# A layer norm, a feed-forward pass and a long convolution on one core: block 0's transposes and first products in halves of 256 rows

## The chip, the core and the metric

The kernel runs on one core of a Trainium2 chip. The metric is device time in microseconds (us) of one execution; for each kernel the median over its runs is compared. The core has a matrix engine (TensorE, PE in the profile, its weight loads PEld), VectorE (DVE), ScalarE (ACT), GpSimd (POOL) and SyncE (SP), each of which works through its own list of instructions strictly in order, and 16 DMA engines. DMAs are issued by SP, ACT or POOL from the same lists.

## What is computed

The input is x (2048 rows of 576 features). With xn = layernorm(x), the result is

```
out = x + q(xn) * y(k, v) + relu(xn @ w1) @ w2        # w1 is 576 x 4608, w2 is 4608 x 576
```

where y is a gated long convolution over the 2048 rows (short shift convolution of k, times v, then a causal convolution of length 2048 done as a transform written in matmuls) and xn gates it. All data are float32. The change concerns only the feed-forward part, relu(xn @ w1) @ w2, in its first microseconds.

## The kernel before, in words

**Precision.** A float32 product is made of three fast passes: each operand is split into a rounded high part (`hi`, `h1`, `hh`, written by ACT) and a low part (the operand minus its high part, written by DVE for activations and by POOL for weights), and high*high, low*high and high*low are summed in PSUM.

**Tiles of the feed-forward part.** The rows are 16 tiles of 128, in 4 blocks of 4 tiles (512 rows). The 4608 hidden features are 12 chunks of 384, each chunk 3 feature tiles j of 128. The loops run over halves of the rows (blocks 0 and 1, then 2 and 3), then chunks `ci`, then the blocks of the half, then j. `mm1` (L323) makes one hidden tile: 14 matmuls of 512 columns into a PSUM tile `psh` (two buffers), from the transposed activations `xhi`, `xlo`, `xhl` and the split weights h, l; then ACT writes `hh` (relu, L333) and DVE `ll` (L334). `mm2` (L340) multiplies the three hidden tiles of a chunk by w2: for each row tile and each half of the 576 output columns 9 matmuls of 288 columns into `pso` (three buffers), added to the accumulator `acc` by DVE (L355 for block 0, with a factor rstd; L359 for the others).

**The convolution** is a generator (`conv`). After a given amount of matmul work `tick` (L719) lets it emit its next few instructions, so that its matmuls stand among those of the feed-forward part.

**The start.** `acc` first holds x itself. Row tiles are loaded in pairs, each pair by two DMAs of 64 partitions (L152). The loads ahead of everything are, in this order: pair 0 (tiles 0, 1) and pair 2 (tiles 2, 3), each with one DMA on SP's queue and one on ACT's; then on SP's queue the first 128 columns of w1's chunk 0 (L282, L284, three DMAs), its other 256 columns (three DMAs), w2's chunk 0 (L292), the pairs of block 1 and the convolution's kernel. A DMA on SP can't be issued before the eighth DMA ahead of it has landed, because eight semaphores go round. 22 + 11 matmuls on a tile of zeros (`keep_warm`, L749) keep PE busy while it has nothing to do.

`first_xT` (L210) prepares block 0. For each of its four row tiles DVE takes the statistics (L168, L169), writes the negated mean (L225), and ACT subtracts the mean (L227; tile 1 is done by DVE, L189); the factor rstd is left to L355. PE transposes each centred tile in five pieces (L233), and when all four row tiles stand in the five PSUM tiles, `split_x` (L200) makes `xhi` and `xlo`/`xhl` for c = 0 to 4, 512 columns at a time. `split_w1` (L294) splits a feature tile of w1: ACT writes h (L301), POOL l (L271). `split_w2` (L303) does the same for w2 (L310, L271). After the first hidden tile, `make_xT` (L242) prepares block 1: statistics, rstd, then (x - mean) * rstd by DVE (L183), transposes (L263), split.

**What sets the order.** Within an engine the order is fixed when the program is built, by a list scheduler with its own estimate of times; `tc.issue_after(i)` only says that what stands inside is not placed ahead of instruction i. PE thus alternates between hidden tiles 0 and 1 from the first product on: the two are finished together, six `pso` matmuls follow, then hidden tile 2.

Of the kernel before, what the change touches and what calls it, by code (L numbers as in the profile page):

```python
# [10 lines left out]
F32 = mybir.dt.float32  # L11
F32R = mybir.dt.float32r
AF = mybir.ActivationFunctionType
OP = mybir.AluOpType
# [23 lines left out]
A2 = U * T  # L38
GR = P // (2 * A2)
NG = A1 // GR  # L40
N_WARM = 22
WARM_TILE = (0, 6, 3, 2)


W_MM1 = 14 * 512
# [63 lines left out]
def h3_ffn_kernel(ctx: ExitStack, tc, x, k, v, shift_k, ssm_k, ssm_D, w1, w2, fwd, inv, mid, out):  # L109
# [76 lines left out]
    def centred(dst, src, t):  # L186


        return nc.vector.tensor_scalar(dst, src, mv[:, t, 0:1], None, op0=OP.subtract)  # L189

    xT = {}
    done = {}

# [3 lines left out]
        hl = xp.tile([P, 512], F32R, tag="xhl", name=f"xhl{b}")  # L197
        xT[b] = (hi, lo, hl)

    def split_x(b, c, ps):  # L200
        hi, lo, hl = xT[b]
        if c < 4:
            nc.scalar.activation(hi[:, c, :], ps, AF.Copy)
            nc.vector.tensor_tensor(lo[:, c, :], ps, hi[:, c, :], OP.subtract)  # L204
        else:
            done["act"] = nc.scalar.activation(hl[:64, :], ps[:64, :], AF.Copy)
            done["dve"] = nc.vector.tensor_tensor(hl[64:, :], ps[:64, :], hl[:64, :],
                                                  OP.subtract)

    def first_xT(srcs):  # L210

        xT_tiles(0)
        ps = []
        for c in range(5):
            ps.append(ps_o.tile([P, 512], F32, tag="o", name=f"psx{c}") if c >= 3 else fft_psum())
        neg = xp.tile([P, BT], F32, tag="neg", name="neg", bufs=1)
        behind = None
        for t in range(BT):
            if t % 2 == 0:
                pair = xp.tile([P, 2, D], F32, tag="xn", name=f"xn{t}", bufs=BT // 2)  # L220
            xn = pair[:, t % 2, :]
            with tc.issue_after(behind.ins) if behind else nullcontext():
                stats(t, srcs[t])
                if t != 1:
                    behind = nc.vector.tensor_scalar(neg[:, t:t + 1], mv[:, t, 0:1], -1.0, None,  # L225
                                                     op0=OP.mult)
                    done["act"] = nc.scalar.activation(xn, srcs[t], AF.Identity,  # L227
                                                       bias=neg[:, t:t + 1])
                else:
                    behind = centred(xn, srcs[t], t)  # L230
            for c in range(5):
                w = min(P, D - c * P)
                nc.tensor.transpose(ps[c][:w, t * P:(t + 1) * P], xn[:, c * P:c * P + w], ident)  # L233
            keep_warm(WARM_TILE[t])
        with tc.issue_after(done["act"].ins):
            split_w1(0, 1)
        for c in range(5):
            split_x(0, c, ps[c])
        with tc.issue_after(done["dve"].ins):
            inv_std(0, BT)  # L240

    def make_xT(b, srcs, in_place=False):  # L242

        xT_tiles(b)
        t0 = b * BT
        with tc.issue_after(done["acc" if in_place else "dve"].ins):
            for t in range(t0, t0 + BT):
                stats(t, srcs[t])
            inv_std(t0, BT)
        xn = []  # L250
        for t in range(t0, t0 + BT):
            if in_place:
                xn.append(srcs[t])
            else:
                if t % 2 == 0:
                    pair = xp.tile([P, 2, D], F32, tag="xn", name=f"xn{t}", bufs=BT // 2)
                xn.append(pair[:, t % 2, :])
            normalized(xn[-1], srcs[t], t)
        for c in range(5):
            w = min(P, D - c * P)  # L260
            ps = fft_psum()
            for i in range(BT):
                nc.tensor.transpose(ps[:w, i * P:(i + 1) * P], xn[i][:, c * P:c * P + w], ident)  # L263
            split_x(b, c, ps)

    def at_turn(ci):
# [48 lines left out]
    hid = {}  # L315
    added = set()

    def mm1(ci, b, j):
        h1, l1, _, _ = weights[ci][j]
        hi, lo, hl = xT[b]  # L320
        ps = ps_h.tile([P, 512], F32, tag="h", name=f"psh{ci}_{b}_{j}")
        seq = []
        for c in range(4):  # L323
            seq += [(h1[:, c, :], hi[:, c, :]), (h1[:, c, :], lo[:, c, :]),
                    (l1[:, c, :], hi[:, c, :])]
        seq += [(h1[:, 4, :], hl), (l1[:, 4, :], hl)]
        for i, (a, m) in enumerate(seq):
            nc.tensor.matmul(ps, a, m, start=i == 0, stop=i == len(seq) - 1)  # L328
            if i % 7 == 6:
                tick(W_MM1 / 2)  # L330
        hh = hp.tile([P, 512], F32R, tag="hh", name=f"hh{ci}_{b}_{j}")
        ll = hp.tile([P, 512], F32R, tag="ll", name=f"ll{ci}_{b}_{j}")
        done["act"] = nc.scalar.activation(hh, ps, AF.Relu)  # L333
        nc.vector.scalar_tensor_tensor(ll, ps, 0.0, hh, op0=OP.max, op1=OP.subtract)  # L334
        hid[ci, b, j] = (hh, ll)

    def mm2(ci, b, i):
        t = b * BT + i
        cols = slice(i * P, (i + 1) * P)
        if ci == HALVES * NCHUNK - 1:  # L340
            while t not in added:
                next(stream)
        for h in range(2):
            ps = ps_o.tile([P, 512], F32, tag="o", name=f"pso{ci}_{t}_{h}")
            dc = slice(h * NH, (h + 1) * NH)
            n = 0
            for j in range(FT):
                hh, ll = hid[ci, b, j]
                _, _, h2, l2 = weights[ci][j]
                for a, m in ((hh, h2), (hh, l2), (ll, h2)):  # L350
                    nc.tensor.matmul(ps[:, :NH], a[:, cols], m[:, dc],  # L351
                                     start=n == 0, stop=n == 3 * FT - 1)
                    n += 1
            if b == 0:
                done["acc"] = nc.vector.scalar_tensor_tensor(  # L355
                    acc[t][:, dc], ps[:, :NH], rstd[:, t:t + 1], acc[t][:, dc],
                    op0=OP.mult, op1=OP.add)
            else:
                done["acc"] = nc.vector.tensor_tensor(acc[t][:, dc], ps[:, :NH], acc[t][:, dc],  # L359
                                                      OP.add)  # L360
            if ci == HALVES * NCHUNK - 1 and t == T - 1:
                for u, queue in ((0, nc.sync), (1, nc.scalar)):
                    queue.dma_start(out[u, :, t, dc], acc[t][halves(u)[0], dc])
            tick(W_MM2 / 2)
        if ci % NCHUNK == NCHUNK - 1:
            if t < HT:
                if t % 2:
                    nc.sync.dma_start(fin[t // 2], pairs[t - 1])
            else:
                if t == T - 2:  # L370
                    move(acc[t], out, t, store=True)
                elif t % 2 and t < T - 1:
                    move(pairs[t - 1], out, slice(t - 1, t + 1), store=True)
# [375 lines left out]
    def keep_warm(n):  # L749
        for i in range(n):  # L750
            nc.tensor.matmul(idle, warm[:, :P], warm, start=True, stop=True)

    keep_warm(N_WARM)
    split_w1(0, 0)
    first_xT(acc)
    for j in range(2, FT):
        with tc.issue_after(done["act"].ins):
# [21 lines left out]
    for half in range(HALVES):  # L779
        for cc in range(NCHUNK):  # L780
            ci = half * NCHUNK + cc
            for bi in range(HB):
                b = half * HB + bi
                if half == 0 and cc == NCHUNK - 1:
                    tl = {}
                    bn = HB + bi
                    for t in range(bn * BT, (bn + 1) * BT, 2):
                        pair = load_x(t, "xn", BT // 2)
                        tl[t], tl[t + 1] = pair[:, 0, :], pair[:, 1, :]
                    make_xT_later = (bn, tl, True)  # L790
# [47 lines left out]
```

## Time and profile before

| | |
|---|---|
| median of 3 runs | 1081.67 us (1080.42 to 1083.54) |
| the profiled execution | 1082.52 us, of which its span, first to last instruction, is 1080.7 us |
| granted clock of PE in the span | 1.000 |
| PE busy in 0 to 20 us, 20 to 40 us | 18.33 us, 18.55 us |
| PE busy in 40 to 60, 60 to 80, 80 to 100 us | 20.00 us each |
| bytes moved by DMA | 150.79 MB, 140 GB/s over the span |

A row of the profile's timeline gives start and length in us, engine, line, operation, `out<-in`, shape and count; in brackets stands how long the engine was idle before and what ended that. A page's groups give busy time and the mean length of one instruction in ns. The busy time of PE counts the length of a matmul, though the next one starts before it ends.

### The profile page before, as it was taken

The numbers are of one execution on the slowest core, as the hardware profiler recorded it, in microseconds if no ns is written. First come the engines' busy times: TensorE is split into PE (matmuls) and PEld (weight loads), VectorE is DVE, ScalarE is ACT, GpSimd is POOL, SyncE is SP. The second block draws the span as 40 slices with busy tenths as digits, with TensorE's granted clock in tenths as the row PEclk, the third lists the DMA queues.
The fourth block names the chain that finished last, engine by engine and source line by source line (L and its number), as shares of the span: only waits on it lengthen the run. The fifth ranks groups of instructions, "written<-read, shape, count | busy, mean of one in ns | idle before, by whom it ended". The sixth has DMA issues, their size and how long they took to land.

```text
span 1080.7 us, 17268 instructions
## 1 busy us (share of the span) xinstructions
PE 1068.9 (99%) x6545; PEld 975.2 (90%) x6545; DVE 728.8 (67%) x1215; ACT 583.2 (54%) x1181; POOL 322.1 (30%) x307
## 2 busy tenths in 40 slices
PE   8999999999999999999999999999999999999998
PEld 5989998989999999999989999899999999999998
DVE  6322787849998767677556575666656656877774
ACT  4221787823442423333387887888788864543430
POOL 4341342423423422412313041312224032442410
PEclk9999999999999999999999999999999999999999
DMA  9960455665545425416644342434344237644524
GB/s 231 182 158 1 149 156 163 196 184 151 178 134 151 150 75 156 126 51 201 187 145 138 97 149 86 136 99 136 97 142 133 86 103 224 203 126 145 170 76 110
DMA packets 99183, 150.79 MB, mean 140 GB/s; under 512 B 45261, under 2 KB 49583, under 8 KB 99100
## 3 DMA queue, kind: packets, MB, share of 16 engines
q1 hardware_dynamic: 79548, 92.87, 29.7%
q0 software_dynamic: 19232, 56.08, 17.7%
q8 instruction: 52, 0.85, 0.3%
q10 hardware_dynamic: 320, 0.74, 0.3%
q14 instruction: 31, 0.25, 0.1%
HBM read 114.26 MB, written 35.39 MB: 138 GB/s over the span
## 4 chain that ended last, share of the span: by engine, by line
PE 90%; DMA 5%; ACT 2%; DVE 2%; issue 1%; SPq 0%; POOL 0%; POOLq 0%; ACTq 0%; DVEq 0%
PE pso L351 39%; PE psh L328 39%; PE psf L555 7%; PE psf L391 3%; DMA r<-in_w 2%; DMA acc<-in_x 1%; PE psf L693 1%; PE psf L694 1%; DMA sk<-in_shift_k 1%; PE psf L263 1%; DMA zk<-zk 1%; DMA k<-in_k 0%; ACT h L310 0%; DVE lok L546 0%; POOL l L271 0%
## 5 line engine op out<-in xcount | busy, mean ns | idle before, releaser
L271 POOL TENSOR_TENSOR l<-r,h 128x640 fp32r<-128x640 f32 (+1 forms) x144 | 225.3, 1569 | 550.3 <-ACT h L301 397.9
L351 PE MATMUL pso<-l,hh 128*128 128x288 f32 x1152 | 338.3, 295 | 0.0
L351 PE MATMUL pso<-h,ll 128*128 128x288 f32 x1152 | 337.8, 295 | 0.0
L351 PE MATMUL pso<-h,hh 128*128 128x288 f32 x1152 | 336.6, 295 | 0.8 <-DVE acc L359 0.6
L328 PE MATMUL psh<-xhi,h 128*128 128x512 f32 x576 | 225.9, 393 | 1.6 <-DVE ll L334 1.2
L328 PE MATMUL psh<-xlo,h 128*128 128x512 f32 x576 | 226.2, 393 | 0.0
L328 PE MATMUL psh<-xhi,l 128*128 128x512 f32 x576 | 225.5, 391 | 0.0
L351 PEld LDWEIGHTS pso<-h,hh 128*128 128x128 f32 x1152 | 215.6, 188 | 7.4 <-DVE acc L359 1.0
L351 PEld LDWEIGHTS pso<-l,hh 128*128 128x128 f32 x1152 | 216.1, 188 | 5.9
L351 PEld LDWEIGHTS pso<-h,ll 128*128 128x128 f32 x1152 | 215.8, 188 | 0.5
L333 ACT ACTIVATE hh<-psh 128x512 fp32r<-128x512 f32 x144 | 85.4, 595 | 173.5 <-PE psh L328 172.8
L359 DVE TENSOR_TENSOR acc<-pso,acc 128x288 f32<-128x288 f32 x288 | 128.4, 451 | 72.1 <-PE pso L351 69.1
L334 DVE SCALAR_TENSOR_TENSOR ll<-psh,hh 128x512 fp32r<-128x512 f32 x144 | 98.9, 687 | 102.6 <-ACT hh L333 102.0
L328 PEld LDWEIGHTS psh<-xhi,l 128*128 128x128 f32 x576 | 108.2, 188 | 20.4
L328 PEld LDWEIGHTS psh<-xhi,h 128*128 128x128 f32 x576 | 108.0, 188 | 17.5 <-DVE ll L334 1.4
L328 PEld LDWEIGHTS psh<-xlo,h 128*128 128x128 f32 x576 | 108.1, 188 | 15.5 <-DVE xlo L204 0.4
L310 ACT ACTIVATE h<-r 128x576 fp32r<-128x576 f32 x72 | 48.6, 681 | 57.1 <-DMA r<-in_w 32.9
L355 DVE SCALAR_TENSOR_TENSOR acc<-pso,rstd,acc 128x288 f32<-128x288 f32 x96 | 48.4, 513 | 33.4 <-PE pso L351 32.7
L392 ACT ACTIVATE zx<-psf 128x288 f32<-128x288 f32 x64 | 25.7, 407 | 61.5 <-PE psf L391 37.5
L385 DVE TENSOR_TENSOR ks<-kt,ks 64x288 fp32r<-64x288 f32 x64 | 57.2, 893 | 2.4 <-ACT ks L384 0.4
L591 DVE TENSOR_TENSOR k<-psf,k 128x288 f32<-128x288 f32 x64 | 29.2, 456 | 42.8 <-ACT sw L590 42.6
L328 PE MATMUL psh<-xhl,l 128*128 128x512 f32 x144 | 56.4, 392 | 0.0
(109 smaller groups left out, 1533.7 us busy)
## 6 DMA issues: line engine op xcount, KB each, us to landing
r<-in_w POOLq DMA_DIRECT2D x23, 864.0 KB, 6.0
r<-in_w POOLq DMA_DIRECT2D x23, 768.0 KB, 6.5
zk<-zk SPq DMA_DIRECT2D x32, 288.0 KB, 2.8
zx<-zx SPq DMA_DIRECT2D x32, 288.0 KB, 3.1
ztk<-zk SPq DMA_DIRECT2D x32, 288.0 KB, 3.1
ztx<-zx SPq DMA_DIRECT2D x32, 288.0 KB, 2.8
zy<-vo SPq DMA_DIRECT2D x32, 288.0 KB, 2.0
zo<-zy SPq DMA_DIRECT2D x32, 288.0 KB, 3.0
```

The source lines that it names most:

```text
L271: return nc.gpsimd.tensor_tensor(dst, src, hi, OP.subtract)
L310: nc.scalar.activation(h2, r2[:, j, :], AF.Copy)
L328: nc.tensor.matmul(ps, a, m, start=i == 0, stop=i == len(seq) - 1)
L333: done["act"] = nc.scalar.activation(hh, ps, AF.Relu)
L334: nc.vector.scalar_tensor_tensor(ll, ps, 0.0, hh, op0=OP.max, op1=OP.subtract)
L351: nc.tensor.matmul(ps[:, :NH], a[:, cols], m[:, dc], start=n == 0, stop=n == 3 * FT - 1)
L355: done["acc"] = nc.vector.scalar_tensor_tensor(acc[t][:, dc], ps[:, :NH], rstd[:, t:t + 1], acc[t][:, dc], op0=OP.mult, op1=OP.add)
L359: done["acc"] = nc.vector.tensor_tensor(acc[t][:, dc], ps[:, :NH], acc[t][:, dc], OP.add)
L385: nc.vector.tensor_tensor(dst[other], src[own], dst[own], OP.subtract)
L391: nc.tensor.matmul(ps[:, :NH], w[:, u, n, :], stk, start=n == 0, stop=n == 1)
L555: nc.tensor.matmul(ps[:, :NH], a, m[:, cols], start=n == 0, stop=n == 2)
L591: nc.vector.tensor_tensor(k1[:, cols], ps, k1[:, cols], OP.mult)
```

## The change

Block 0 is handled in two halves of 256 rows. In each half two row tiles are centred and transposed, the five PSUM tiles are split 256 columns at a time, and the products of hidden tiles 0 and 1 (`N_EARLY = 2`) for those 256 columns are made: 14 matmuls of 256 columns for each, high-weight products first and low-weight products (which need POOL's l) last. `mm1` then finds these two `psh` tiles ready and only writes hh and ll.

- In a half, the first row tile is centred by DVE (statistics, then subtract); the second by ACT alone, which sums the row in one pass with an accumulated output and subtracts in a second one. Its statistics, still needed for rstd, are taken by DVE later.
- Pair 0 alone is loaded ahead of w1. Pair 2 is issued on SP's queue between the first 128 and the other 256 columns of w1's chunk 0 (inside `load_w1`).
- h of feature tile 0 is split behind tile 1's centring; h of feature tile 1 behind the third high part (c = 2) of the first half; w1's third feature tile and w2's three come after the second half, as before.
- There are 21 + 2 matmuls on zeros instead of 33.
- Block 1 (`second_xT`) is prepared after hidden tile 1 instead of hidden tile 0. Its statistics follow the first low part `ll`; its tiles are centred only, by ACT with a negated mean from DVE, and rstd is left to `mm2`, so that L355's form of the addition (L414 in the changed kernel) serves block 1 too.
- Blocks 2 and 3 keep `make_xT`, in place.

```diff
-N_WARM = 22
-WARM_TILE = (0, 6, 3, 2)
+N_WARM = 21
+N_EARLY = 2
...
+    def centre(dst, src, t, how, behind=None):
+        if how != "dve":
+            neg = xp.tile([P, 1], F32, tag="neg", name=f"neg{t}", bufs=4)
+        with tc.issue_after(behind.ins) if behind else nullcontext():
+            if how == "act":
+                nc.scalar.activation(dst, src, AF.Copy, scale=-1.0 / D, accum_out=neg)
+            else:
+                stats(t, src)
+                if how == "dve":
+                    return nc.vector.tensor_scalar(dst, src, mv[:, t, 0:1], None,
+                                                   op0=OP.subtract)
+                last = nc.vector.tensor_scalar(neg, mv[:, t, 0:1], -1.0, None, op0=OP.mult)
+            act = nc.scalar.activation(dst, src, AF.Identity, bias=neg)
+        return act if how == "act" else last
...
     def first_xT(srcs):
...
+        xn = row_pairs(0)
+        behind = {0: None, 1: None}
+        for half in range(2):
+            cols = slice(256 * half, 256 * half + 256)
+            for i in range(2):
+                t = 2 * half + i
+                last = centre(xn[t], srcs[t], t, ("dve", "act")[i], behind[i])
+                if t == 0:
+                    with tc.issue_after(last.ins):
+                        stats(1, srcs[1])
+                transposes(ps, xn[t], t)
+            if half == 0:
+                keep_warm(2)
+                with tc.issue_after(last.ins):
+                    split_w1(0, 0)
             for c in range(5):
...
+                high, low = split_x(0, c, ps[c], cols)
+                if half == 0 and c == 2:
+                    behind[0] = low
+                    with tc.issue_after(high.ins):
+                        split_w1(0, 1)
+            behind[1] = high
+            for j in range(N_EARLY):
+                if half == 0:
+                    early[j] = ps_h.tile([P, 512], F32, tag="h", name=f"psh0_0_{j}")
+                products(0, 0, j, early[j], cols)
+        with tc.issue_after(low.ins):
+            stats(3, srcs[3])
+
+    def second_xT(srcs):
+        xT_tiles(1)
+        with tc.issue_after(lows[0].ins):
             inv_std(0, BT)
+        xn = row_pairs(BT)
+        last = lows[1]
+        for i in range(BT):
+            last = centre(xn[i], srcs[BT + i], BT + i, "both", last)
...
+            split_x(1, c, ps)
+        with tc.issue_after(last.ins):
+            inv_std(BT, BT)
...
     def load_w1(ci):
...
+            if step == P:
+                load_acc(2)
...
+    def products(ci, b, j, ps, cols=None):
...
+        if cols is None:
+            seq = [p for c in range(5) for p in (*highs[2 * c:2 * c + 2], rests[c])]
+        else:
+            seq = highs + rests
         for i, (a, m) in enumerate(seq):
-            nc.tensor.matmul(ps, a, m, start=i == 0, stop=i == len(seq) - 1)
+            to, m = (ps, m) if cols is None else (ps[:, cols], m[:, cols])
+            nc.tensor.matmul(to, a, m, start=i == 0, stop=i == len(seq) - 1)
...
+    def mm1(ci, b, j):
+        if ci == b == 0 and j in early:
+            ps = early[j]
+            tick(W_MM1)
...
-            if b == 0:
+            if b < HB:
                 done["acc"] = nc.vector.scalar_tensor_tensor(
...
-    for t in range(0, BT, 2):
-        load_acc(t, queues=(nc.sync, nc.scalar))
+    load_acc(0, queues=(nc.sync, nc.scalar))
...
-                    if (ci, b, j) == (0, 0, 0):
-                        make_xT(1, acc)
+                    if (ci, b, j) == (0, 0, 1):
+                        second_xT(acc)
```

More of the change, by code (lines that the diff above doesn't have):

```diff
@@ L215, in first_xT @@
             ps.append(ps_o.tile([P, 512], F32, tag="o", name=f"psx{c}") if c >= 3 else fft_psum())
[L216 to L230, printed above, removed]
-            for c in range(5):
-                w = min(P, D - c * P)
-                nc.tensor.transpose(ps[c][:w, t * P:(t + 1) * P], xn[:, c * P:c * P + w], ident)
-            keep_warm(WARM_TILE[t])
@@ L235, in first_xT @@
[L235 to L239, printed above, removed]
-            inv_std(0, BT)
[L242 to L258, printed above, removed]
+        xn = row_pairs(0)
@@ L263, in make_xT @@
                 nc.tensor.transpose(ps[:w, i * P:(i + 1) * P], xn[i][:, c * P:c * P + w], ident)
+            split_x(1, c, ps)
+        with tc.issue_after(last.ins):
+            inv_std(BT, BT)
+    def make_xT(b, srcs):
+        xT_tiles(b)
+        t0 = b * BT
+        with tc.issue_after(done["acc"].ins):
+            for t in range(t0, t0 + BT):
+                stats(t, srcs[t])
+            inv_std(t0, BT)
+        for t in range(t0, t0 + BT):
+            normalized(srcs[t], srcs[t], t)
+        for c in range(5):
+            w = min(P, D - c * P)
+            ps = fft_psum()
+            for i in range(BT):
+                nc.tensor.transpose(ps[:w, i * P:(i + 1) * P], srcs[t0 + i][:, c * P:c * P + w],
+                                    ident)
             split_x(b, c, ps)
@@ L333, in mm1 @@
         done["act"] = nc.scalar.activation(hh, ps, AF.Relu)
-        nc.vector.scalar_tensor_tensor(ll, ps, 0.0, hh, op0=OP.max, op1=OP.subtract)
+        lows.append(nc.vector.scalar_tensor_tensor(ll, ps, 0.0, hh, op0=OP.max,
+                                                   op1=OP.subtract))
         hid[ci, b, j] = (hh, ll)
@@ L753, in h3_ffn_kernel @@
     keep_warm(N_WARM)
-    split_w1(0, 0)
     first_xT(acc)
```

45 lines of the change are left out of this document (28 added, 17 removed).

## The prediction

> **What bounds the kernel now.** I read the page's busy times first, then the windows, then the timeline of the start.
>
> ```profile
> span 1080.7 us, 17268 instructions
> PE 1068.9 (99%) x6545; PEld 975.2 (90%) x6545; DVE 728.8 (67%) x1215; ACT 583.2 (54%) x1181; POOL 322.1 (30%) x307
> ```
>
> PE is the bound: 11.8 us of the span are not its own. What happens ahead of the steady stretch is worth what it moves that stretch, and the change works only there. The timeline of the start:
>
> ```profile
> 1.20 8.74 PE L751 MATMUL psw<-warm 128*128 128x512 bf16 x32 [1.20 <-DVE table L745]
> 4.59 4.85 PEld L751 LDWEIGHTS <-warm 128*128 128x128 bf16 x23 [0.27 <-issue]
> 6.08 0.82 DVE L168 BATCH_NORM_STATS2 bn<-acc 128x6 f32<-128x288 f32 x2 [4.93 <-DMA acc<-in_x]
> 6.93 0.21 DVE L169 BATCH_NORM_AGGREGATE mv<-bn 128x2 f32<-128x12 f32 x1
> 8.34 0.52 DVE L189 TENSOR_SCALAR xn<-acc,mv 128x576 f32<-128x576 f32 x1
> 8.66 0.37 SPq L292 DMA_DIRECT2D r<-in_w  x1
> 9.92 0.74 ACT L301 ACTIVATE h<-r 128x640 fp32r<-128x640 f32 x1 [1.78 <-DMA r<-in_w]
> 10.56 1.43 ACT L227 ACTIVATE xn<-acc,neg 128x576 f32<-128x576 f32 x2
> 11.90 0.72 ACT L301 ACTIVATE h<-r 128x640 fp32r<-128x640 f32 x1
> 12.53 1.54 ACT L203 ACTIVATE xhi<-psf 128x512 fp32r<-128x512 f32 x3
> 12.70 1.56 POOL L271 TENSOR_TENSOR l<-r,h 128x640 fp32r<-128x640 f32 x1 [0.41 <-ACT h L301]
> 13.13 1.89 DVE L204 TENSOR_TENSOR xlo<-psf,xhi 128x512 fp32r<-128x512 f32 x3 [1.96 <-ACT xhi L203]
> 13.15 0.74 PE L328 MATMUL psh<-xhi,h 128*128 128x512 f32 x2 [0.34 <-ACT xhi L203]
> 15.54 1.83 ACT L310 ACTIVATE h<-r 128x576 fp32r<-128x576 f32 x3
> 15.73 4.35 POOL L271 TENSOR_TENSOR l<-r,h 128x640 fp32r<-128x640 f32 x3 [1.47 <-ACT h L301]
> 19.65 1.09 ACT L333 ACTIVATE hh<-psh 128x512 fp32r<-128x512 f32 x2 [2.07 <-PE psh L328]
> 20.30 0.40 PE L351 MATMUL pso<-h,hh 128*128 128x288 f32 x1 [0.23 <-ACT hh L333]
> 21.84 0.68 DVE L334 SCALAR_TENSOR_TENSOR ll<-psh,hh 128x512 fp32r<-128x512 f32 x1
> 22.58 0.50 PE L328 MATMUL psh<-xhi,h 128*128 128x512 f32 x1 [1.22 <-DVE ll L334]
> ```
>
> Products start at 13.15 us, hidden tiles 0 and 1 end near 20, and hidden tile 2 waits until 22.58 for `ll`, which frees its PSUM buffer. Up to there the two kernels do the same: the transposes of block 0, 28 products, six `pso` matmuls. So I compare one moment: **the first product of hidden tile 2, at 22.58 us before**. From then on the chain of waits is PE alone:
>
> ```profile
> 22.58 3.47 PE psh L328 x14
> 26.04 1.59 PE pso L351 x12
> 27.64 1.31 PE psf L263 x12
> 28.95 1.20 PE pso L351 x9
> 43.46 3.20 PE psh L328 x14
> ```
>
> These also give prices: 3.20/14 = 0.229 us for a matmul of 512 columns, 1.59/12 = 0.133 for 288, 1.31/12 = 0.109 for a transpose. A straight line through the first two gives 0.119 for 256 columns; the 288-column price 0.133 is the upper bound, half of 0.229 the lower. I take 0.119 (only 32 columns away from a measured one): the 56 half products then cost 6.7 us against 28 x 0.229 = 6.4.
>
> **When the data come.** SP's windows (clock, DMA share, GB/s at the end of a row):
>
> ```profile
> 2.00:4.00 2.00, 1.00 0.92 226
> 4.00:6.00 2.00, 1.00 1.06 242
> 6.00:8.00 2.00, 1.00 1.03 202
> 8.00:10.00 2.00, 1.00 1.15 302
> 10.00:12.00 2.00, 1.00 1.08 346
> ```
>
> The DMA engines are full throughout, so what counts is the order of the bytes. A pair of x is 0.59 MB, w1's first part 0.33, its second 0.66. Before: two pairs and the first part, 1.51 MB, are through at 8.5 us, and ACT could use them at 9.92 (1.78 us of idle until a DMA), a lag of about 1.3 us. With the second part it is 2.16 MB, through at 10.6, usable about 11.8; ACT's next split of w1 at 11.90 shows no DMA wait. After: pair 0 first, as before, usable at 6.08; w1's first part behind 0.92 MB, through at 5.9, usable at about 7.2 instead of 9.9; pair 2 behind 1.51 MB, usable at about 9.8; **w1's second part behind the same 2.16 MB, so again at about 11.8**. SP's three DMAs of that part and pair 2's two are issued several us before their turn; w2's load, issued at 8.66 before, when pair 2 had landed, now waits for w1's first part instead (7.2) and has 2.16 MB ahead of it either way.
>
> **The first half.** DVE: statistics 6.08 to 7.14, subtraction to about 7.7 (0.52, L189). ACT beside it: a pass that sums, then a pass that subtracts. Before shows no accumulating pass; its bounds are the 681 ns of a plain 128x576 ACTIVATE (below) and twice that; I take 0.70, near the plain one. The second pass is 0.76 (two in 1.43, overlapping): done at 7.6, at the upper bound at 8.3, when PE is still transposing tile 0. The matmuls on zeros run at 0.42 us until 4.59, then at 0.21 (4.85/23), so 23 end at about 7.8; ten transposes end at 8.9. The ten matmuls left out filled idle time and bring nothing by themselves.
>
> ```profile
> L310 ACT ACTIVATE h<-r 128x576 fp32r<-128x576 f32 x72 | 48.6, 681 | 57.1 <-DMA r<-in_w 32.9 <-PE pso L351 24.1
> L392 ACT ACTIVATE zx<-psf 128x288 f32<-128x288 f32 x64 | 25.7, 407 | 61.5 <-PE psf L391 37.5 <-issue 21.6 <-ACT h L310 1.2
> ```
>
> A high part of 256 columns costs ACT, in a row, between half of 0.51 (1.54/3, 512 columns) and 0.41 (288 alone); I take 0.31, a low part on DVE 0.37 (half of 1.89/3 is 0.32, L359 below takes 0.45 for 288). ACT's order in the changed program is: the two passes, h of tile 0, high parts c = 0, 1, 2, **h of tile 1**, high parts c = 3, 4, two passes for row tile 3, five high parts of the second half, h of tile 2, w2's three h, then hh. So h of tile 0 runs 7.7 to 8.4, three high parts 8.7 to 9.7, and then ACT stands until w1's second part lands at 11.8. **This is the wait that takes the place of the old ones.** Queued behind it on ACT are c = 3 and 4 and all of the second half; behind those low parts on DVE, the subtraction of row tile 2 (whose statistics wait for pair 2 only); on PE, five products of tile 0 are done at 10.1, and the next in its list needs h of tile 1. From 10.1 to 12.55 PE has nothing.
>
> **From 11.8 to the moment compared.** h of tile 1 to 12.5 (0.72). PE: 19 half products at 0.119, to 14.8 (POOL's l of tile 1, 12.6 + 1.56 = 14.2, is needed at 14.4). ACT ends c = 4 at 13.2, row tile 3's passes at 14.7; DVE ends row tile 2 at 14.4: both in time. Ten transposes to 15.9; the first PSUM tile is whole at 15.6. ACT: five high parts 15.7 to 17.2, h of tile 2 to 17.9, w2's three (1.83) to 19.7, hh at 19.6 to 20.2. PE follows the low parts (last at 18.0) and ends its 28 at about 19.4, so it waits for hh: the `pso` matmuls begin at 20.25, as before (20.30). Three run; the other three need w2's first l. POOL: l of tile 2 from 17.95, then that l, 1.55 + 1.4 (4.35 for three): 20.95. They end at 21.4. `ll` has freed the buffer by 20.9. **Hidden tile 2 starts at 21.4 instead of 22.58: 1.2 us.** The stall of 1.22 us goes because DVE no longer has block 1's statistics ahead of `ll`; late next are POOL's l and ACT's w2 splits.
>
> **Block 1.** DVE now does, between 21 and 28: second `ll`, four statistics, four negated means, third `ll`; ACT two tiles (23.2 to 25.5) before hh, two behind it. PE's first six transposes (due 26.2) find theirs; the last three (due 28.3) wait for the fourth tile, which DVE's queue (statistics of 1.05 and `ll` 0.7) gives at about 28.6: 0.3 us. DVE's four L183 (2.2 us) leave. Between no loss and 0.35, the gain is 0.85 to 1.2; **I take 1.0.**
>
> **Costed at nothing.** L355's form for block 1 (rows: 513 against 451 ns, 96 more) is 6 us of DVE in 1080, hidden behind PE (DVE busy 67%); without cover 6 us. POOL is 2.4 us later with w1's next chunk: its split stood for 16 us. Two ticks fewer only move convolution steps.
>
> ```profile
> L359 DVE TENSOR_TENSOR acc<-pso,acc 128x288 f32<-128x288 f32 x288 | 128.4, 451 | 72.1 <-PE pso L351 69.1
> L355 DVE SCALAR_TENSOR_TENSOR acc<-pso,rstd,acc 128x288 f32<-128x288 f32 x96 | 48.4, 513 | 33.4 <-PE pso L351 32.7
> 41.52 4.63 POOL L271 TENSOR_TENSOR l<-r,h 128x640 fp32r<-128x640 f32 x3 [16.16 <-ACT h L301]
> ```
>
> The profiled execution was 1082.52 us (span 1080.7 and 1.8 around it), 0.85 above the median. It becomes 1081.5, and the median of 1081.67 becomes **1080.7 us**.
>
> **Rivals.**
>
> *A: ACT does not wait for w1's second part.* If it were there by 9.7, h of tile 1 would run 9.65 to 10.4, the high parts end at 11.0, row tile 2 on DVE at 12.6, the transposes at 13.7, the second half at 17.3, and hidden tile 2 would start at about 19.2: a gain of 3.4, **1078.3**. For it: weights move at 302 to 346 GB/s, pairs of x at 202 to 242. Against it: 2.16 MB must be through, whatever their order, and were not before 10.6.
>
> *B: PE's clock drops in the hole; slower than before.* Between 7.8 and 12.55 PE has ten transposes and five half products. At the start it took 3.4 us (1.20 to 4.59) of matmuls at 0.42 us until they came at 0.21. If that returns once, 3.4 us at half speed from 12.55 delay the first half's end by 1.7, and all behind it: 1.7 - 1.0, **1082.4**. If it lasts two such periods, 3.4 are lost: **1084.1**. It decides if so little work in 4.7 us counts as idle. Against it: before, from 9.8 to 13.15, PE also had only transposes and one matmul on zeros, and the 28 products behind came at full speed (13.15 to 20, 28 x 0.229 = 6.4). For it: that stretch was shorter and denser. [...]
>
> *C: the later order.* The scheduler moves convolution steps everywhere. PE's waits behind 60 us are
>
> ```profile
> PE psf L555 <- ACT k L579: 1.7, 3, 0.8
> PE psf L391 <- ACT zk L392: 1.5, 1, 1.5
> PE psf L555 <- DVE k L591: 0.7, 2, 0.6
> PE pso L351 <- DVE acc L359: 0.6, 1, 0.6
> ```
>
> 4.5 us in sum; all gone is 1076.2, all doubled 1085.2. No row says which way.
>
> **Chances.** Forecast 0.52, A 0.20, B 0.16, C 0.12 (half each way). A measurement of this kernel tells about 0.3% from no change, 3.2 us: faster means below 1078.4, slower above 1084.9. A lies on the first edge (0.12 of it beyond), C's halves add 0.06 each, B's upper part with noise 0.05: faster 0.18, within 0.71, slower 0.11. The likeliest case alone reaches from 1079.5 to 1082; with A and most of B the range is 1077.8 to 1084.2.
>
> **What would show it.** ACT's split of feature tile 1 (L345) idle for about 2 us until a DMA, starting near 11.8; 256-column matmuls 0.119 apart; the first product of hidden tile 2 near 21.4, `pso` held by POOL just ahead of it. Under A that split starts before 10.5 and hidden tile 2 near 19; under B half products come 0.21 or more apart behind 12.5. I am wrong if the second part lands elsewhere than at 11.8, if an accumulating pass takes over 1.4 us, or if waits behind 60 us change by more than 2 us.

## The result, and the profile after

| | median | runs |
|---|---|---|
| before | 1082.16 us | 1080.42 to 1083.6, 6 runs |
| after | 1087.86 us | 1085.01 to 1090.29, 6 runs |

The ratio is 1.0051, 95% interval 1.0041 to 1.0061: the changed kernel is **slower by 5.7 us**, where 1.0 us of gain had been forecast. The profiled execution of after is the fastest of the six, 1085.01 us at a mean granted clock of 1.000; the other five show 0.998 or 0.999, which matters below.

The page of the profile after:

```profile
span 1083.2 us, 17328 instructions
PE 1068.6 (99%) x6563; PEld 976.1 (90%) x6563; DVE 746.0 (69%) x1218; ACT 587.1 (54%) x1193; POOL 320.1 (30%) x307
L414 DVE SCALAR_TENSOR_TENSOR acc<-pso,rstd,acc 128x288 f32<-128x288 f32 x192 | 96.6, 511 | 45.8 <-PE pso L410 44.2
L410 PE MATMUL pso<-h,hh 128*128 128x288 f32 x1152 | 336.5, 295 | 3.9 <-DVE acc L414 3.9
L418 DVE TENSOR_TENSOR acc<-pso,acc 128x288 f32<-128x288 f32 x192 | 85.6, 451 | 39.7 <-PE pso L410 38.1
```

PE is as busy as before, to 0.3 us; the span is 2.5 us longer. The third and fourth rows hold one of the causes already: 96 more additions in the form with rstd, and `pso` matmuls that were idle for 3.9 us behind just that form. The timeline of the start of after, in part:

```profile
6.12 0.68 ACT L215 ACTIVATE xn<-acc 128x576 f32<-128x576 f32 x1 [3.30 <-DMA acc<-in_x]
6.71 0.19 ACT L215 ACTIVATION_READ_ACCUMULATOR xn<-acc 128x1 f32 x1
6.93 0.78 ACT L222 ACTIVATE xn<-acc,neg 128x576 f32<-128x576 f32 x1
10.23 0.28 PE L378 MATMUL psh<-xhi,h 128*128 128x256 f32 x1
11.66 0.74 ACT L345 ACTIVATE h<-r 128x640 fp32r<-128x640 f32 x1 [1.94 <-DMA r<-in_w]
12.45 0.39 PE L378 MATMUL psh<-xhi,h 128*128 128x256 f32 x1 [1.94 <-ACT h L345]
18.31 4.35 POOL L313 TENSOR_TENSOR l<-r,h 128x640 fp32r<-128x640 f32 x3 [4.26 <-ACT h L345]
20.48 0.66 PE L410 MATMUL pso<-h,hh 128*128 128x288 f32 x3
21.32 0.66 PE L410 MATMUL pso<-l,hh 128*128 128x288 f32 x3 [0.18 <-POOL l L313]
21.82 0.39 PE L378 MATMUL psh<-xhi,h 128*128 128x512 f32 x1
```

The start went as forecast: ACT waits 1.94 us for w1's second part until 11.66, PE has nothing from 10.51 to 12.45 (below: **the hole**), and hidden tile 2 starts at 21.82 instead of 22.58. The chain of waits (start, length, what; in part) names the same pieces; the 4.23 us of "issue" are POOL's idle time ahead of 18.31, which the timeline ends by ACT's h:

```profile
6.05 5.54 DMA r<-in_w
11.66 0.74 ACT h L345
12.47 1.57 POOL l L313
14.04 4.23 issue
18.31 2.97 POOL l L313 x2
21.32 0.66 PE pso L410 x3
21.99 3.20 PE psh L378 x14
25.18 1.58 PE pso L410 x12
```

So the time is lost behind the start. To see where, I took from each trace the end of ACT's `hh` of each of the 144 hidden tiles, and subtracted the same tile's end in before. The profiled after stands like this: -0.3 us at hidden tile 2 (26.7 us in before; PE's last product of that tile is 0.9 early, but `hh` stands behind ACT's centring of block 1), -0.9 at 89 us, -2.5 at 223 us, then **+1.9 at 346 us**, +1.6 at 511 us, +2.5 at the last tile, 1063 us. PE's waits behind 60 us in after (us in sum, times, longest):

```profile
PE pso L410 <- DVE acc L414: 3.9, 4, 1.6
PE psf L614 <- ACT k L638: 1.2, 3, 0.5
PE psf L614 <- DVE k L650: 1.1, 3, 0.6
PE psf L614 <- issue: 0.7, 1, 0.7
```

The first row, all between 223 and 346 us, is most of the 4.4 us lost there: before had one such wait of 0.6. Windows of that stretch (busy us of PE, PEld, DVE, ACT, POOL in 20 us), first before, then after:

```profile
280.00:300.00 20.00, 20.00 (x122) 18.23 (x121) 18.23 (x23) 9.23 (x18) 9.52 (x10) 1.00 0.66 197
300.00:320.00 20.00, 20.00 (x124) 18.24 (x123) 19.70 (x29) 6.26 (x13) 4.46 (x4) 1.00 0.43 130
```

```profile
280.00:300.00 20.00, 18.37 (x114) 16.70 (x112) 18.26 (x21) 6.68 (x13) 8.29 (x10) 1.00 0.63 181
300.00:320.00 20.00, 19.04 (x114) 16.99 (x113) 19.67 (x32) 8.20 (x17) 3.67 (x4) 1.00 0.44 136
```

DVE is 91 and 99% busy here in both kernels, not 67%: it makes the convolution's short products (`c`, `e`) beside the additions. Before, PE had no gap all the same; after, it has. That was to be seen in before's page, in the line of DVE's busy tenths (40 slices of 27 us; the tenth to twelfth are the stretch from 243 to 324 us):

```profile
DVE  6322787849998767677556575666656656877774
```

The timeline of after shows what the largest wait hangs on:

```profile
288.21 0.50 DVE L414 SCALAR_TENSOR_TENSOR acc<-pso,rstd,acc 128x288 f32<-128x288 f32 x1
289.42 4.44 DVE L539 TENSOR_TENSOR c<-c,e 128x576 f32<-128x576 f32 x1
289.84 1.44 POOL L313 TENSOR_TENSOR l<-r,h 128x576 fp32r<-128x576 f32 x1
291.79 1.44 POOL L313 TENSOR_TENSOR l<-r,h 128x576 fp32r<-128x576 f32 x1
294.68 0.76 DVE L539 TENSOR_TENSOR c<-c,e 128x576 f32<-128x576 f32 x1
295.96 0.51 DVE L414 SCALAR_TENSOR_TENSOR acc<-pso,rstd,acc 128x288 f32<-128x288 f32 x1
296.52 0.40 PE L410 MATMUL pso<-h,hh 128*128 128x288 f32 x1 [1.63 <-DVE acc L414]
```

One product of DVE takes 4.44 us instead of 0.76, while POOL does two subtractions. The addition behind it comes 7.7 us after the one before, all three `pso` buffers are full, and PE stands.

### The profile page after: what moved, and what is told of

Same layout as the page of the kernel before. It is cut to its first block, busy times and chain, and to the rows that moved or that the text cites. A ratio compares the mean times of both kernels' runs of the same rounds, so it can differ in the third digit from the quotient of the medians.

```text
span 1083.2 us, 17328 instructions
## 1 busy us (share of the span) xinstructions
PE 1068.6 (99%) x6563; PEld 976.1 (90%) x6563; DVE 746.0 (69%) x1218; ACT 587.1 (54%) x1193; POOL 320.1 (30%) x307
## 4 chain that ended last, share of the span: by engine, by line
PE 78%; DVE 8%; ACT 6%; DMA 4%; issue 2%; POOL 0%; SPq 0%; ACTq 0%; POOLq 0%
PE psh L378 34%; PE pso L410 34%; PE psf L614 5%; PE psf L450 3%; DVE c L539 1%; DVE e L538 1%; DVE k L667 1%; DMA ztx<-zx 1%; DVE acc L414 1%; DMA sk<-in_shift_k 1%; PE psf L752 1%; PE psf L753 1%; ACT k L637 1%; DVE k L663 1%; ACT k L638 1%
## 5 line engine op out<-in xcount | busy, mean ns | idle before, releaser
L378 PE MATMUL psh<-xhi,h 128*128 128x512 f32 (+1 forms) x584 | 226.6, 390 | 2.0 <-ACT h L345 1.9
L378 PE MATMUL psh<-xlo,h 128*128 128x512 f32 (+1 forms) x584 | 227.2, 391 | 0.1
L378 PE MATMUL psh<-xhi,l 128*128 128x512 f32 (+1 forms) x584 | 224.8, 388 | 0.0
L414 DVE SCALAR_TENSOR_TENSOR acc<-pso,rstd,acc 128x288 f32<-128x288 f32 x192 | 96.6, 511 | 45.8 <-PE pso L410 44.2
L418 DVE TENSOR_TENSOR acc<-pso,acc 128x288 f32<-128x288 f32 x192 | 85.6, 451 | 39.7 <-PE pso L410 38.1
L605 DVE TENSOR_TENSOR lok<-ztk,hik 128x576 fp32r<-128x576 f32 x32 | 27.3, 853 | 48.1 <-ACT hik L604 48.1
L345 ACT ACTIVATE h<-r 128x640 fp32r<-128x640 f32 x72 | 52.5, 732 | 7.6 <-DMA r<-in_w 7.3
```

What stands on the lines that cost most here:

```text
L345: nc.scalar.activation(h1, r1[:, :, cols], AF.Copy)
L378: nc.tensor.matmul(to, a, m, start=i == 0, stop=i == len(seq) - 1)
L414: done["acc"] = nc.vector.scalar_tensor_tensor(acc[t][:, dc], ps[:, :NH], rstd[:, t:t + 1], acc[t][:, dc], op0=OP.mult, op1=OP.add)
```

## The experiments

Three theories came out of the result, and each has its edit. **D**: block 1's additions with rstd keep DVE from freeing the `pso` buffers in time. **H**: the hole lowers PE's clock. **T**: the two half ticks that `mm1` leaves out for hidden tiles 0 and 1 put the convolution's steps in worse places. "+x" is the median less that of before beside it (1082.06 us for a_again to e3, 1081.62 for e4 to e7, 1082.37 for e8 to e11, 1082.62 for e12 to e14).

**a_again**, the changed kernel itself.

> The changed kernel once more, unchanged, to see how its executions spread. Theory H (the hole): in most executions PE's clock falls to half speed in the hole from 10.2 to 12.45 us and stays low for one or more periods of some 3.4 us; then about 4 executions in 5 show a mean granted clock of 0.998 and 1087 to 1090 us, the rest 1.000 and 1085, and a profile with 0.998 has products of 256 columns more than 0.2 us apart behind 12.5. Theory D (DVE): the loss sits behind 60 us, where PE waits for DVE's additions, 3 us and more in every profile, and no product of the start is slow.

1088.93 us, **+6.9**, ratio 1.0064 (1.005 to 1.0077). The profiled execution took 1091.7 us. Its windows, with the granted clock as the third number from the end:

```profile
10.00:12.50 2.50, 0.94 (x5) 0.60 (x4) 1.51 (x5) 0.22 (x1) 0.47 (x1) 1.00 1.08 323
12.50:16.00 3.50, 2.66 (x12) 2.66 (x13) 1.58 (x4) 2.71 (x6) 1.55 (x1) 0.50 1.08 305
16.00:19.40 3.40, 3.40 (x18) 3.37 (x17) 0.00 (x0) 0.00 (x0) 0.00 (x0) 0.51 1.10 209
19.40:25.00 5.60, 5.31 (x39) 4.45 (x37) 3.83 (x11) 4.96 (x12) 3.11 (x3) 1.00 1.50 138
```

PE runs at half clock from 12.53 to 19.36 us, out of the hole: rival B, twice as long as its lower case. Hidden tile 2 ends 3.3 us late instead of 0.3 early, and the 3.6 us between this execution and the profiled one of after are still there at the end (6.7 by then).

**e1_fill**, the hole filled with matmuls on zeros.

```diff
+N_FILL = 11
+N_FILL_AT = 4
...
+            if i == N_FILL_AT and fill is not None:
+                with tc.issue_after(mm.ins):
+                    for _ in range(N_FILL):
+                        nc.tensor.matmul(fill, warm[:, :P], warm, start=True, stop=True)
```

> The changed kernel with 11 matmuls on zeros (2.4 us) put on PE behind the fifth half product, so that the hole is filled and nothing else moves. Theory H: every execution has a granted clock of 1.000, the median falls from about 1088 to about 1085. Theory D: the median stays at 1087 to 1088.

1090.8 us, **+8.7**, ratio 1.0077 (1.0064 to 1.0089), above what either theory gave. The clock is 1.000 in all five executions, so the hole is what lowers it; but the time doesn't fall. As the only cause, H falls. The edit isn't clean either: PE's list also changed order between 48 and 77 us.

**e2_late**, h of feature tile 1 behind row tile 3, and its first half of products behind those of tile 0's.

```diff
-                    with tc.issue_after(high.ins):
-                        split_w1(0, 1)
+            if half == 1:
+                with tc.issue_after(last.ins):
+                    split_w1(0, 1)
+                early[1] = ps_h.tile([P, 512], F32, tag="h", name="psh0_0_1")
+                products(0, 0, 1, early[1], slice(0, 256))
```

> The changed kernel with h of feature tile 1 split behind row tile 3's centring, so that ACT doesn't stand for w1's second part with c = 3 and 4 and row tile 3 behind it. Both theories: hidden tile 2 starts 0.8 to 1.2 us earlier than the 21.8 us of the changed kernel. Theory H: the hole shrinks to about 1.2 us (11.4 to 12.6), the clock stays at 1.000, median 1083.5 to 1085. Theory D: 1086 to 1087.5.

1086.22 us, **+4.2**, ratio 1.0046 (1.0033 to 1.006), clock 0.999 or 1.000. In its timeline ACT no longer waits for w1, and PE's longest idle there is 0.55 us:

```profile
12.14 0.38 PE L381 MATMUL psh<-xlo,h 128*128 128x256 f32 x1 [0.55 <-DVE xlo L199]
12.36 0.72 ACT L348 ACTIVATE h<-r 128x640 fp32r<-128x640 f32 x1
```

**e3_norm**, block 1 normalised by DVE and added plainly as before, at the changed kernel's place.

```diff
-        for i in range(BT):
-            last = centre(xn[i], srcs[BT + i], BT + i, "both", last)
+        with tc.issue_after(lows[1].ins):
+            for i in range(BT):
+                stats(BT + i, srcs[BT + i])
+            inv_std(BT, BT)
+        for i in range(BT):
+            normalized(xn[i], srcs[BT + i], BT + i)
...
-            if b < HB:
+            if b == 0:
```

> The changed kernel with block 1 normalised by DVE as in the kernel before (rstd applied at once, the plain addition of 451 ns in place of 511 for block 1), at the new place. Theory D: the waits for DVE behind 60 us fall from 3.9 us to about 0.6 and the median by about 3 us, to 1085. Theory H: the median stays near 1088, most executions at 0.998, and only the waits for DVE change.

1085.92 us, **+3.9**, ratio 1.0038 (1.0026 to 1.0051). The waits between 223 and 346 us are gone; one of 2.0 us for a DMA of the convolution (`ztk`) is new at 534 us.

**e4_ticks**, two half ticks.

```diff
-            tick(W_MM1)
+            tick(W_MM1 / 2)
+            tick(W_MM1 / 2)
```

> The changed kernel with two ticks of half the work for each early hidden tile, as the kernel before had, so that the convolution's middle stage stands again behind the same feed-forward matmul as before (in the changed kernel it stands some 30 matmul rows, about 11 us, earlier). Theory T (ticks): the waits of PE between 520 and 560 us shrink from some 3 us to the 2 us of before and the median falls by 1 to 3 us, to 1085.5 to 1087. Theory P (phase): what is lost behind 500 us only depends on when everything arrives there, and the median stays near 1088.5.

1086.63 us, **+5.0**, ratio 1.0045 (1.0033 to 1.0057).

**e5_late_norm**, the edits of e2 and e3 together.

> Feature tile 1's split behind row tile 3 together with block 1 normalised by DVE as before (the plain addition). Hole and additions both gone: if the two losses add, the clock stays at 1.000, PE no longer waits for DVE's additions around 250 to 303 us, and the median is 1082.5 to 1084. If the losses behind 500 us grow in their place (theory P) it stays at 1085 to 1086.

1083.6 us, **+2.0**, ratio 1.0022 (1.001 to 1.0034).

**e6_late_norm_ticks**, all three.

> The same with the ticks of before as well. Theory T: the later part is that of before, and only the earlier start is left: 1080 to 1081.5. Theory P: 1082.5 to 1085, with new waits elsewhere.

1080.89 us, **-0.7**, ratio 0.9993 (0.9984 to 1.0001): with the three undone, the changed start alone is as fast as before, or hardly faster.

**e7_before_b1**, the kernel before with block 1 centred and its additions with rstd.

```diff
-            normalized(xn[-1], srcs[t], t)
+            if in_place:
+                normalized(xn[-1], srcs[t], t)
+            else:
+                centred(xn[-1], srcs[t], t)
...
-            if b == 0:
+            if b < HB:
```

> The kernel before with one part of the change alone: block 1 is only centred (by DVE), and its additions take the form with rstd (511 ns in place of 451). Theory D: PE waits about 4 us for these additions between 230 and 310 us, median 1084.5 to 1086.5, clock 1.000. If the additions cost this only together with the rest of the change: 1081.5 to 1083.

1088.98 us, **+7.4**, ratio 1.0068 (1.0056 to 1.008), more than expected. In the profiled execution 3.2 us are lost by hidden tile 2, because here DVE's centring stands ahead of `ll`, and 4.4 us between 223 and 346, with the waits

```profile
PE pso L354 <- DVE acc L358: 2.9, 3, 1.8
```

and 3.41 us at half clock behind the last of them, at 300.4 us (its mean granted clock is 0.998). So the old kernel pays for this form of addition too.

**e8_norm_ticks** (the hole stays), **e9_late_ticks** (rstd stays), **e10_fill_norm_ticks** (e8 with the filler) and **e11_before_ticks** (before, with the ticks of after):

> The changed kernel with two of the three suspects undone: block 1 is normalised by DVE and added plainly, and the two early hidden tiles tick twice by half each; the hole (h of feature tile 1 ahead of the end of the first half) stays. If the three causes simply add, as the runs so far suggest (2.3 to 2.7 us for the ticks, 2.6 to 3.0 for block 1's additions, 2.7 for the hole), this is 1088.9 - 2.5 - 2.8, about 1083.6, with a mean clock of 0.997 to 0.998 in most executions. If the hole costs nothing by itself and only made the other two worse, it is 1081, as the version with all three undone (1080.9).

> The changed kernel with h of feature tile 1 behind row tile 3 (no hole) and two half ticks; block 1's additions keep the factor rstd. If the causes add: 1088.9 - 2.7 - 2.5, about 1083.7, with PE waiting about 3 to 4 us for DVE's additions between 230 and 310 us. If the additions cost only together with the shifted steps of the convolution: about 1081.

> As e8_norm_ticks, and the hole filled by 11 matmuls on zeros, which keep the clock at 1.0 but leave hidden tile 2 as late as with the hole. If the hole costs by the clock: 1 to 2.5 us less than e8_norm_ticks, 1081.3 to 1082.5. If it costs by the shifted times alone and not by the clock: as e8_norm_ticks, within 0.5 us.

> The kernel before with one edit: hidden tiles 0 and 1 of chunk 0 tick once for the whole tile and not twice by half each, so that the convolution's steps stand earlier among the matmuls, as in the changed kernel. If the earlier steps cost by themselves: 1081.6 + 2.5, about 1084. If they cost only together with the other parts of the change: 1081.6 to 1082, no difference.

| | median | | ratio |
|---|---|---|---|
| e8_norm_ticks | 1083.64 | **+1.3** | 1.0015 (1.0005 to 1.0025) |
| e9_late_ticks | 1084.01 | **+1.6** | 1.0014 (1.0005 to 1.0022) |
| e10_fill_norm_ticks | 1084.42 | **+2.1** | 1.0014 (1.0004 to 1.0023) |
| e11_before_ticks | 1085.53 | **+3.2** | 1.0026 (1.0016 to 1.0035) |

All eight combinations of the three edits are there now, and **they add**. Undoing block 1's part (e3's edit) gains 3.0, 2.2, 3.7 and 2.4 us in its four pairs, the ticks' 1.9, 2.5, 2.6 and 2.7, the hole's 2.7, 1.9, 3.4 and 2.0. Each cause is thus worth about the same with and without the others, to within 1.5 us. (The means sum to 7.7 us, and from a_again to e6 it is 7.6; but these two agree almost by construction.) The filler again brings nothing (e10 against e8), though the clock is 0.999 or 1.000 in all its executions.

e11 shows the ticks alone. Its wait, and its windows around 535 us:

```profile
PE psf L558 <- DMA ztk<-zk: 2.7, 1, 2.7
```

```profile
535.00:538.00 3.00, 0.38 (x3) 0.14 (x1) 1.35 (x3) 0.60 (x1) 2.01 (x2) 1.00 0.98 358
538.00:540.00 2.00, 1.89 (x10) 1.82 (x11) 0.94 (x2) 1.85 (x4) 1.40 (x3) 0.72 0.97 381
540.00:542.00 2.00, 2.00 (x8) 1.71 (x7) 0.18 (x1) 1.91 (x6) 0.00 (x0) 0.50 1.04 417
```

Two ticks fewer put the convolution's middle stage (`psf<-hik`) 24 matmuls earlier in PE's order: PE comes to it at 535.4 us, in before at 539.0, without a wait. (The 11 us in the expectation of e4 were too many.) At 535.4 its DMA (`ztk`) hasn't landed: PE waits until 538.1, and half clock follows.

e3, e5, e6, e8 and e10 had changed two things at once in block 1, the centring and the form of the addition. The last three runs part them:

```diff
 e12_plain: changed kernel, e13_late_ticks_plain: e9
-            if b < HB:
+            if b == 0:
 e14_act_norm: e6
+            shift = xp.tile([P, BT], F32, tag="shift", name="shift1")
+            nc.vector.scalar_tensor_tensor(shift, mv[:, BT:2 * BT, 0], -1.0,
+                                           rstd[:, BT:2 * BT], op0=OP.mult, op1=OP.mult)
...
-            normalized(xn[i], srcs[BT + i], BT + i)
+            nc.scalar.activation(xn[i], srcs[t], AF.Identity, bias=shift[:, i:i + 1],
+                                 scale=rstd[:, t:t + 1])
```

> The changed kernel with one edit: block 1's additions are the plain ones, so the factor rstd of block 1 is left out of the computation; its centring by ACT stays. If the form of the addition is the cause: no addition waits of 1 us and more between 223 and 346 us, no DVE operation c<-c,e of over 4 us, about 4 us less than the changed kernel (1088.4), so 1084.4. If the other parts of block 1's preparation are the cause: 1088.

> e9_late_ticks (no hole, two half ticks) with the plain additions and so without the factor rstd of block 1. If the form is the cause: 1084.0 - 3 to 4, about 1080.3; with the 1.7 us that centring gained over normalising by DVE between 27 and 89 us it comes out below e6_late_norm_ticks (1080.9), near 1079.5. If the preparation is the cause: 1084.

> e6_late_norm_ticks (no hole, two half ticks, plain additions) with block 1 normalised by ACT in one pass (scale rstd, added -mean*rstd) in place of DVE's four subtract-and-multiply; nothing is left out. If the 1.7 us between 27 and 89 us were DVE's queue: 1079.2 to 1080, faster than before by about 2 us. If they were the wait for rstd, which this version has too: 1080.9 as e6_late_norm_ticks.

| | median | | ratio |
|---|---|---|---|
| e12_plain | 1085.95 | **+3.3** | 1.0022 (1.0011 to 1.0034) |
| e13_late_ticks_plain | 1080.01 | **-2.6** | 0.9972 (0.9962 to 0.9983) |
| e14_act_norm | 1081.43 | **-1.2** | 0.9985 (0.9976 to 0.9995) |

**The form alone** is worth 3.5 us (a_again to e12) and 4.3 us (e9 to e13). The two windows of e12 that answer to those above are full again:

```profile
280.00:300.00 20.00, 20.00 (x123) 18.34 (x122) 18.23 (x23) 9.31 (x18) 9.38 (x10) 1.00 0.69 200
300.00:320.00 20.00, 20.00 (x123) 18.34 (x123) 19.70 (x28) 6.25 (x12) 4.49 (x4) 1.00 0.43 130
```

e14 is the one version that computes everything and is faster than before, by 0.05 to 0.24%. Whether it also beats e6 (0.9993) isn't settled, as their intervals overlap.

Where each profiled execution, one of each kernel, gains (-) and loses (+) against before, by the ends of `hh`, in us (the columns' limits are times in before; * marks a granted clock of 0.5 for 3.41 us or more in that column):

| | to 27 | 27-89 | 89-223 | 223-346 | 346-511 | 511-1063 |
|---|---|---|---|---|---|---|
| after | -0.3 | -0.7 | -1.6 | **+4.4** | -0.3 | +1.0 |
| a_again | +3.3* | -0.5 | -1.0 | **+4.6** | -0.3 | +3.1 |
| e1_fill | +0.4 | -0.5 | -0.9 | **+5.2** | -0.3 | +4.7 |
| e2_late | -1.1 | -0.6 | -1.3 | **+4.4** | -0.3 | +1.6 |
| e4_ticks | +1.8* | -0.6 | -1.3 | **+3.5*** | 0.0 | -0.4 |
| e9_late_ticks | -0.8 | -0.6 | -1.0 | **+4.2** | 0.0 | -0.2 |
| e7_before_b1 | +3.2 | -1.5 | -1.5 | **+4.4*** | +0.1 | +1.7 |
| e3_norm | -0.3 | +1.1 | -1.7 | +0.2 | -0.3 | +3.2* |
| e5_late_norm | -1.3 | +1.1 | -1.0 | +0.1 | -0.3 | +2.0 |
| e6_late_norm_ticks | -2.1 | +1.1 | -0.7 | +1.3 | 0.0 | -0.1 |
| e8_norm_ticks | +1.1* | +1.1 | -0.6 | +2.7* | 0.0 | +1.0 |
| e10_fill_norm_ticks | -0.3 | +1.1 | -0.7 | +0.8 | 0.0 | +0.5 |
| e11_before_ticks | +0.6 | 0.0 | -0.6 | +0.6 | -0.3 | +5.3* |
| e12_plain | +1.9* | -0.7 | -1.2 | +0.4 | -0.3 | +3.6 |
| e13_late_ticks_plain | -1.2 | -0.6 | -0.6 | +0.3 | 0.0 | -0.1 |
| e14_act_norm | -1.4 | +1.0 | -1.3 | -0.4 | 0.0 | +1.2 |

The fourth column splits by the form of the addition: 4.2 to 5.2 us in six of the seven kernels with rstd in block 1, at most 1.3 in the others but for e8. In e4 (with rstd) and e8 (plain) the loss has another source. In e4:

```profile
237.81 0.76 DVE L539 TENSOR_TENSOR e<-k-1_2459,sk 128x576 f32<-128x576 f32 x1 [6.71 <-DMA k-1_2459<-in_k]
241.32 0.40 PE L411 MATMUL pso<-h,hh 128*128 128x288 f32 x1 [2.61 <-DVE acc L415]
```

The addition that PE waits for stands in DVE's list behind a product whose DMA is late, and half clock follows (`pso` matmuls 0.24 us apart from 242.02 on, 0.13 before). e6, e8 and e10, with plain additions and the same two ticks, have this wait as well (2.0, 1.8 and 1.5 us), and in e8 half clock follows too (a granted clock of 0.61 and 0.54 in 242 to 244 and 244 to 246 us). The last column leans by the ticks, with an overlap: 1.0 to 5.3 where two are missing, -0.4 to 1.7 where they stand. In the kernels that centre block 1 with ACT, `hh` of hidden tile 2 comes about 0.6 us late for its products, so that 0.6 us of their second column belong to the first.

## Why the prediction was wrong

**The start: right.** w1's second part was to be usable at 11.8, ACT took it at 11.66; the hole was to last from 10.1 to 12.55 and did from 10.51 to 12.45; half products were to be 0.119 us apart and are 0.12; the accumulating pass was to cost 0.70 and takes 0.68, and 0.19 more for reading the accumulator, which I hadn't counted. `pso` came at 20.48 (20.25), and hidden tile 2 at 21.82 (21.4): behind POOL, as said, 0.4 late. In an execution without half clock, 0.76 of the 1.2 us were there.

**Block 1's preparation: right.** "Between no loss and 0.35": no loss. PE's last product of hidden tile 2 ends 0.86 us earlier than before, and the lead is 0.92 at 89 us. (The 0.5 to 0.7 of the table's second column are no gain of PE: in before it has no wait between 26 and 89 us.) Normalising at the same place loses 1.0 to 1.1 (e3, e5, e6, e8, e10), by ACT as well (e14). That points to the wait for rstd, which both have, and not to DVE's four operations.

**"Costed at nothing": this step failed.** The form of block 1's additions was put at 6 us "hidden behind PE (DVE busy 67%)". That share is a mean over the kernel. From 243 to 324 us DVE is nine tenths busy or more, and the additions there free the `pso` buffers that PE waits for next. The 46 additions with rstd between 225 and 345 us in e2 and e9, half of them block 1's, are 23 x 0.06 = 1.4 us more work for DVE; the loss is 3.5 to 4.3. The rest seems to come from where DVE's products then fall beside POOL's work: over the same 740 matmuls of PE (220 to 347 us in e9, to 344 in e13) DVE is busy 109.9 us in e9 and 106.9 in e13, 1.4 of it for the additions, 4.0 more for `c<-c,e` and 2.6 less for `c<-c,v`. The mean `c<-c,e` between 240 and 340 us, before and after:

```profile
L480 DVE TENSOR_TENSOR c<-c,e 128x576 f32<-128x576 f32 x23 | 21.2, 923 | 0.5
```

```profile
L539 DVE TENSOR_TENSOR c<-c,e 128x576 f32<-128x576 f32 x22 | 24.9, 1130 | 0.4
```

One product of 4.43 to 4.46 us stands in after, a_again, e1, e2, e7 and e9; in before and in all versions with plain additions the longest is 2.2 us. e4's profiled execution has the form with rstd and no such product, and PE's only wait there is the one for the late DMA: in it the form shows no cost of its own, though by the medians e4 and e8 differ by 3.7 us. So the form's cost is shown, by e12 and e13, and e7 agrees; that it must take the way of that one product is not. The prediction did give the price without cover, 6 us, but as no rival, and its range didn't reach there.

**"Two ticks fewer only move convolution steps": this failed too.** They move them ahead of their data. That is 1.9 to 2.7 us in the changed kernel and 3.2 in the old one. The DMA that is late was to be looked for: the stage that moves reads what an earlier one writes.

**Rival B: underweighted, at 0.16.** Half clock out of the hole shows in four of the six profiled executions that have it unfilled (a_again, e4, e8 and e12; not after and e3), and 3.41 us at half clock put PE 1.7 us back. What the hole costs in all is 1.9 to 3.4 us. How much of this is the clock stays open: filling the hole restored the clock and not the time, twice, with an edit that also moved other matmuls; and among e12's twelve executions those at a mean clock of 0.999 to 1.000 took 1081.2 to 1084.0 us and those at 0.997 took 1086.1 to 1087.1, but the one of e8 at 1.000 was not faster (1084.4) than those at 0.998.

**Rival A** didn't happen, as argued (11.66). **Rival C** was on the right track and had no direction; the windows of DVE between 240 and 340 us would have given it one. The prediction's sign for it came: PE's waits behind 60 us went from 4.5 us to 6.9, by more than the 2 us named.

**Where the 5.7 us are**: by the medians, the three causes sum to 7.7 us, and the changed start without them (e6) is 0.7 faster than before; a_again stands at 6.9. The one execution of after at full clock has lost 2.5: 2.5 gained until 223 us, 4.4 lost until 346, 0.7 more behind. Of the gain 0.9 is the forecast one; most of the other 1.6 is luck, as before's wait of 1.5 us for `zk`, at 167 us, no longer occurs. The other five executions of after are 2.3 to 5.3 us slower than this one. Half clock can be a part of that, 1.7 us for each 3.41 us of it, but that it is all of it isn't shown: a_again took 1088.0 us in an execution at 1.000.

## What to carry to other kernels

Before an edit is costed at nothing because an engine has time to spare, read that engine's busy share in the stretches where the edit's instructions run, above all where they free a buffer that the bounding engine waits for. A mean of 67% held a stretch of 80 us at over 90%. And where a change shifts a hand-timed sequence, even by two ticks, look for what the moved stage reads: the data may not be there.

## What the runs showed of the hardware

**Half clock came in stretches of 3.4 us.** By the windows it lasted 3.4 us in e8 (behind the hole, and again between 242 and 246 us), in e11 (from 538 us) and in e12 (behind the hole), and in a_again 6.83 us (12.53 to 19.36), twice as long. Full clock lasted 1075.20 us in before (from 4.59 us on) and 1078.61 us in after (from 3.89 us on): 315 and 316 times 3.4133 us.

The length of a gap alone doesn't decide. PE's idle 1.31 us in e8 (11.56 to 12.88), 1.78 us in e4 and 2.32 us in a_again were followed by half clock, with products of 256 columns 0.21 us apart (in e8 from 13.9 us on); after's 1.94 us (10.51 to 12.45) and e3's 2.17 us were not, with products 0.12 us apart. What decides is not shown. after and a_again are the same kernel: the same hole led to half clock in one execution and not in the other (3.6 us apart at hidden tile 2), and this is one reason why executions of a kernel differ. It is not the only one: e1's five, all at 1.000, took 1088.2 to 1092.0 us.

**DVE's products and POOL's subtractions delay each other.** The convolution's products (`c`, `e`, 128x576, both factors in SBUF) between 225 and 345 us, in before and after: with no subtraction of POOL beside it one takes 0.74 to 0.76 us (96 of 136). One that starts while a subtraction of POOL runs ends 0.61 to 0.63 us after POOL's end, whatever is left of that (27 of 28; the other 0.70): 0.94 us of overlap gave 1.56, 1.26 gave 1.88, 1.52 gave 2.14. One that starts first mostly takes its 0.75 us, and POOL's subtraction ends 1.3 to 1.4 us behind it (10 of 12), up to 2.14 us long where 1.43 to 1.58 are usual. But the one of 4.44 us had started 0.42 us ahead of POOL's and still ended behind the second of two in a row (POOL's to 293.23, its own end at 293.86), 3.7 us later than alone; why is not shown.
